# Seven block products for the up layer of a fused attention and maxout kernel, in half-batch units interleaved with the down layer

## The chip, the cores and the metric

One core of one Trainium2 chip. The metric is device time in microseconds (us) of the whole program, launch to end. A profile shows a span about 2 us shorter, from the first to the last instruction.

PE is the matmul engine (PEld its weight loads), DVE the vector engine, ACT the scalar engine, POOL the engine that issues loads, SP the queue that issues stores and transposes.

A bank is a piece of PSUM, the memory that PE writes to; here it holds 128 x 512 numbers of fp32. A relief is the copy, relu or add on ACT or DVE that reads a finished product out of its bank, so that PE can write there again. A g sum or an x sum is one of the sums of blocks that the scheme below makes beforehand, of the up layer's output (g) or of x. A row is one line of a profile view.

## The reference, cut to what matters

```
k_proj = E @ k;  v_proj = F @ v                # per batch (8) and head (8); seq 1024, head_dim 64
attn   = softmax(q @ k_proj.T / 8) @ v_proj    # k_proj has 64 rows
x      = attn, heads side by side              # 8192 x 512
out    = max(x @ w1, x @ w2) @ w_out           # w1, w2: 512 x 1024; w_out: 1024 x 512
```

Both kernels use max(h1, h2) = h2 + relu(h1 - h2). So they make wd = w1 - w2 and m = w2 @ w_out once, and compute out = relu(x @ wd) @ w_out + x @ m. The first factor is the up layer, the rest the down layer.

## The kernel before

A batch is 1024 tokens. The up layer is plain: for each half batch and each of eight column blocks, four matmuls with 512 columns into one of four PSUM banks, then a relu into `gt`.

```python
def up_slots(t, j, banks=None, on_act=()):
    for fb in range(NFB):                                   # 8
        def up(fb=fb):
            h_ps = mm_bank(...)
            for r in range(NDC):                            # 4
                nc.tensor.matmul(out=h_ps, lhsT=wd_sb[:, r, fb * 128 : (fb + 1) * 128],
                                 rhs=t["xt"][:, r, :, j * W : (j + 1) * W], ...)
            # fb in on_act: relu on ACT; otherwise on DVE
        yield up
```

The down layer of batches 1 to 7 already uses a block scheme (Strassen's, in Winograd's form): the product of two 2 x 2 block matrices with seven block products instead of eight, for sums of blocks made beforehand on DVE (`step_s`) and sums of results made afterwards. Each of two groups goes through seven products of twelve matmuls with 256 columns. A product adds onto the bank that holds an earlier one, after that one has been copied out:

```python
def keep(g, name, bank):
    x = ppool.tile([128, 512], FP32, tag="p", name="p_sb")
    nc.scalar.copy(out=x, in_=bank)
order = (p1, 0), (p2, 0), (p1, 1), (p2, 1), (p5, 0), (p6, 0), (p3, 0), (p7, 0), (p5, 1), \
    (p4, 0), (p6, 1), (p3, 1), (p7, 1), (p4, 1)
```

In a batch all up products come first, then all down products. The next batch's attention is cut into small steps (`step_sc` scores, `step_da` sums and weighted values, four pairs of heads) between them. `step_da` issues on ACT a logarithm and, straight after, an exponential that makes the inverse of the softmax sums; the multiply on DVE comes one product later.

The softmax here doesn't subtract the row's maximum and nothing guards it: scores larger than these inputs give would overflow.

Of the kernel before, what the change touches and what calls it, by code (L numbers as in the profile page):

```python
# [16 lines left out]
def kernel(  # L17
# [33 lines left out]
    xpool = ctx.enter_context(tc.tile_pool(name="xpool", bufs=2))  # L51
    gpool = ctx.enter_context(tc.tile_pool(name="gpool", bufs=1))
# [13 lines left out]
    def att_banks():  # L66
        return ps.tile([128, 2, 512], FP32, tag="att", bufs=2, name="att_ps")
# [102 lines left out]
    def step_kv(t, h0=0, h1=H, which="kv", bank=None):  # L170
        kv_ps = mm_bank(n=bank)
# [23 lines left out]
    def step_kpt(t, h0=0, h1=H, n=None):  # L195
        kpt_ps = mm_bank(FP16, n)
        for h in range(h0, h1):
            for r in range(2):
                nc.tensor.transpose(  # L199
                    out=kpt_ps[r * D : (r + 1) * D, (h - h0) * KP : (h - h0 + 1) * KP],  # L200
                    in_=t["kp"][:, h, :],
                    identity=ident16[:KP, :KP],
                )
        nc.vector.tensor_copy(
            out=t["kpt"][:, h0:h1, :].rearrange("q h k -> q (h k)"),
            in_=kpt_ps[:, 0 : (h1 - h0) * KP],
        )
# [44 lines left out]
    def step_da(t, p):  # L252
# [18 lines left out]
        nc.scalar.activation(out=ld, in_=ld, func=ACTF.Exp, scale=-1.0)  # L271
        rec = ld

        def finish():
            nc.vector.tensor_tensor(  # L275
                out=t["xt"][:, p, :, :], in0=at_ps, in1=rec, op=ALU.mult
            )

        return finish
# [69 lines left out]
    def up_slots(t, j, banks=None, on_act=()):  # L349
        t["gt", j] = gt = gpool.tile([128, NFB, HALF], FP16, tag=f"gt{j}", name="gt_sb")  # L350
        for fb in range(NFB):
            def up(fb=fb):
                h_ps = mm_bank(n=None if banks is None else banks[fb % 4])
# [7 lines left out]
                if fb in on_act:  # L361
                    nc.scalar.activation(out=gt[:, fb, :], in_=h_ps, func=ACTF.Relu)  # L362
                else:
                    nc.vector.tensor_scalar_max(gt[:, fb, :], h_ps, 0.0)  # L364
# [68 lines left out]
    NK = NFB // 2 + NDC // 2  # L433
    CH = DM // 2

    def a_block(t, j, h, n):
        if n < NFB // 2:
            return t["gt", j][:, h * NFB // 2 + n, :].rearrange("q (o n) -> q o n", o=2)
        return t["xt"][:, h * NDC // 2 + n - NFB // 2, :, j * W : (j + 1) * W]

    def b_block(h, c):
        def chunk(n):
            cols = slice(c * CH, (c + 1) * CH)
            if n < NFB // 2:
                return wo_sb[:, h * NFB // 2 + n, cols]
            return m_sb[:, h * NDC // 2 + n - NFB // 2, cols]
        return chunk

    T_sb = const.tile([128, 4, NK, CH], FP16)

    def step_t(part):
        if part == 0:
            n0, n1, src = 0, NFB // 2, wo_sb
        else:
            n0, n1, src = NFB // 2, NK, m_sb
        hs = n1 - n0
        blk = lambda h, c: src[:, h * hs : (h + 1) * hs, c * CH : (c + 1) * CH]
        T = [T_sb[:, i, n0:n1, :] for i in range(4)]
        for out_, x, y in (
            (T[0], blk(0, 1), blk(0, 0)),  # L460
            (T[1], blk(1, 1), T[0]),
            (T[2], blk(1, 1), blk(0, 1)),
            (T[3], blk(1, 0), T[1]),
        ):
            nc.vector.tensor_tensor(out=out_, in0=x, in1=y, op=ALU.subtract)


    def step_s(t, which, part):
        if "S" not in t:
            t["S"] = [  # L470
                big(i)[:, 0 : NK * HALF].rearrange("q (n o m) -> q n o m", n=NK, o=2)
                for i in range(4)
            ]
        if part == 0:
            n0, n1 = 0, NFB // 2
            blk = lambda j, h: t["gt", j][:, h * n1 : (h + 1) * n1, :].rearrange(
                "q n (o m) -> q n o m", o=2)
        else:
            n0, n1 = NFB // 2, NK
            hs = NDC // 2  # L480
            blk = lambda j, h: t["xt"][:, h * hs : (h + 1) * hs, :, j * W : (j + 1) * W]
        S = [x[:, n0:n1, :, :] for x in t["S"]]
        for i in which:
            x, y, op = (
                (blk(1, 0), blk(1, 1), ALU.add),
                (S[0], blk(0, 0), ALU.subtract),
                (blk(0, 0), blk(1, 0), ALU.subtract),
                (blk(0, 1), S[1], ALU.subtract),
            )[i]
            for n in range(n1 - n0) if part else (slice(0, n1 - n0),):  # L490
                nc.vector.tensor_tensor(out=S[i][:, n], in0=x[:, n], in1=y[:, n], op=op)  # L491

    def down_steps(b, t):
        A = lambda j, h: lambda n: a_block(t, j, h, n)
        Sb = lambda i: lambda n: t["S"][i][:, n, :, :]
        Tb = lambda i: lambda n: T_sb[:, i, n, :]
        prods = {
            1: (A(0, 0), b_block(0, 0)), 2: (A(0, 1), b_block(1, 0)), 3: (Sb(3), b_block(1, 1)),
            4: (A(1, 1), Tb(3)), 5: (Sb(0), Tb(0)), 6: (Sb(1), Tb(1)), 7: (Sb(2), Tb(2)),
        }  # L500
        st = [{}, {}]

        def product(g, k, name, first):
            if first:
                st[g][name] = mm_bank(n={"X": (0, 2), "Y": (1, 3), "Z": (1, 3)}[name][g])
            bank = st[g][name]
            a, w_ = prods[k]
            for i in range(2):
                for n in range(NK):
                    nc.tensor.matmul(  # L510
                        out=bank[:, i * CH : (i + 1) * CH],
                        lhsT=a(n)[:, g, i * 128 : (i + 1) * 128],
                        rhs=w_(n),
                        start=(first and i == 0 and n == 0), stop=(n == NK - 1), skip_group_check=True,
                    )
            return bank

        def keep(g, name, bank):
            x = ppool.tile([128, 512], FP32, tag="p", name="p_sb")
            nc.scalar.copy(out=x, in_=bank)  # L520
            st[g][name] = x
# [4 lines left out]
        def o_tile(g, j):  # L526
            st[g]["o", j] = opool.tile([128, 2, DM], FP32, tag="o", name="o_sb")

        def add(g, j, c, x, y):
            nc.vector.tensor_tensor(  # L530
                out=cols(st[g]["o", j], c), in0=two(x), in1=two(y), op=ALU.add)

        def store(g, j):
            nc.sync.dma_start(
                out=out.rearrange("(n p i o) m -> n o p i m", p=128, i=NI, o=2)[
                    b, g, :, 2 * j : 2 * j + 2, :
                ],
                in_=st[g]["o", j],
            )

        def p1(g):
            keep(g, "s1", product(g, 1, "X", True))

        def p2(g):
            bank = product(g, 2, "Y", True)
            o_tile(g, 0)
            add(g, 0, 0, bank, st[g]["s1"])

        def p5(g):
            keep(g, "s5", product(g, 5, "Z", True))  # L550

        def p6(g):
            keep(g, "u2", product(g, 6, "X", False))

        def p3(g):
            add(g, 0, 1, product(g, 3, "Z", False), st[g]["u2"])
            store(g, 0)

        def p7(g):
            keep(g, "u3", product(g, 7, "X", False))  # L560
            o_tile(g, 1)
            add(g, 1, 1, st[g]["u3"], st[g]["s5"])

        def p4(g):
            bank = product(g, 4, "X", False)
            nc.scalar.copy(out=cols(st[g]["o", 1], 0), in_=two(bank))  # L566
            store(g, 1)

        order = (p1, 0), (p2, 0), (p1, 1), (p2, 1), (p5, 0), (p6, 0), (p3, 0), (p7, 0), (p5, 1), \
            (p4, 0), (p6, 1), (p3, 1), (p7, 1), (p4, 1)  # L570
        return [lambda f=f, g=g: f(g) for f, g in order]

# [54 lines left out]
    for b in range(1, B):  # L627
        t = tiles[b]
        banks = None if b == 1 else (0, 1, 3, 2)
        seq = [*up_slots(t, 0, banks, (2, 6)), *up_slots(t, 1, banks, (2, 6))]  # L630
        seq += down_steps(b, t)
        own = [((b, n), x) for n, x in enumerate(seq)]
        if b > 1:
            last = slots.pop()
            own[2:2] = [last]
        slots += own
# [3 lines left out]
    def at_slot(b, n, s, *a):  # L640
        steps.setdefault((b, n), []).append(lambda: s(*a))

    for b in range(1, B):
        t = tiles[b]
        at = lambda n, s, *a: at_slot(b - 1, n, s, t, *a)
        if b == 1:
            at(19, new_attn)
            plan = "kv 19, kpt 20, qt0 21, qt1 23, sc0 24, da0 26, qt2 27, sc1 29, da1 31, " \
                "qt3 32, sc2 33, da2 35, sc3 37, da3 39"
        elif b == 2:  # L650
            at_slot(0, 33, new_attn, t)
            at_slot(0, 33, step_qt_dma, t, 0, H // 2)
            at_slot(0, 36, step_qt_dma, t, H // 2, H)
            plan = "kv 1, kpt 2, sc0 4, da0 6, sc1 8, da1 10, sc2 12, da2 14, sc3 16, da3 19"
        else:
            at_slot(b - 2, 7, new_attn, t)
# [67 lines left out]
```

## Time and profile before

| | before |
|---|---|
| time | 357.81 us median of 3 (356.91 to 358.63) |
| span of the profile | 354.6 us, of a run of 356.39 us |
| period of a batch | 39.37 us |
| PE, DVE, ACT busy in a period | 39.13, 25.45, 20.62 us |
| wait of PE in a period | one, 0.24 us |

The period is read from equal places of successive batches in the chain that ended last (167.71, 207.08, 246.45). A PE that is busy 39.13 of 39.37 us says that only fewer or shorter matmuls can help, and that any wait the change adds counts in full.

### The profile page before, as it was taken

The page shows a single profiled execution, that of the slowest core. Times are in us where ns is not written, and L with a number is a line of the kernel's source. Part 1 is how long each engine was busy: PE and PEld are TensorE (multiplying, and loading weights), DVE is VectorE, ACT ScalarE, POOL GpSimd, SP SyncE. Part 2 cuts the span into 40 slices and gives each one's busy share as a digit, 9 for nine tenths or more (in the row PEclk, how much of TensorE's full clock was granted, in tenths as well). Part 3 has the DMA queues.
Part 4 walks back from the last instruction along what each step waited for, and adds up shares of the span by engine and source line. Part 5 has one row for each costly group of instructions (what it writes and reads, how often), then busy time and mean ns, then how long its engine had stood idle before and what let it go on. Part 6 is the DMA issues. An engine that isn't in the chain of part 4 may idle for free.

```text
span 354.6 us, 6214 instructions
## 1 busy us (share of the span) xinstructions
PE 343.9 (97%) x2667; PEld 203.2 (57%) x2667; DVE 209.9 (59%) x312; ACT 169.5 (48%) x219; POOL 31.4 (9%) x43
## 2 busy tenths in 40 slices
PE   8998999999999999999999999999999999999994
PEld 3544444434368644875368635874377635874783
DVE  1367707326894469734992579635972589538911
ACT  2438123772755376536564376436663375432131
POOL 8332001002000100010000100000000000000000
PEclk9999999999999999999999999999999999999999
DMA  8999999999996999849973897869502210031014
GB/s 151 205 195 202 207 207 183 247 152 235 200 204 92 248 255 167 116 134 197 234 118 95 164 254 119 118 154 219 105 2 98 82 59 2 33 146 59 2 66 173
DMA packets 65068, 52.31 MB, mean 148 GB/s; under 512 B 26000, under 2 KB 56720, under 8 KB 65040
## 3 DMA queue, kind: packets, MB, share of 16 engines
q0 software_dynamic: 31312, 28.31, 52.6%
q1 hardware_dynamic: 33728, 23.60, 24.9%
q8 instruction: 21, 0.34, 0.4%
q14 instruction: 7, 0.06, 0.1%
HBM read 57.15 MB, written 16.78 MB: 208 GB/s over the span
## 4 chain that ended last, share of the span: by engine, by line
PE 88%; DMA 4%; DVE 3%; POOL 2%; ACT 1%; issue 1%; DVEq 0%; POOLq 0%
PE mm_ps L510 37%; PE mm_ps L355 31%; PE mm_ps L384 6%; DMA big<-in_moe_w_dram 4%; PE mm_ps L178 4%; PE att_ps L263 3%; PE att_ps L239 3%; PE mm_ps L424 2%; DVE o_sb L530 1%; PE mm_ps L199 1%; DVE gt_sb L364 1%; PE mm_ps L215 1%; POOL q_sb L100 0%; POOL v_sb L100 0%; DVE wd_sb L402 0%
## 5 line engine op out<-in xcount | busy, mean ns | idle before, releaser
L355 PE MATMUL mm_ps<-xt_sb,wd_sb 128*128 128x512 f16 x512 | 119.9, 380 | 1.6 <-DVE wd_sb L402 1.1
L355 PEld LDWEIGHTS <-wd_sb 128*128 128x128 f16 x512 | 46.7, 98 | 63.6 <-issue 13.6
L364 DVE TENSOR_SCALAR gt_sb<-mm_ps 128x512 f16<-128x512 f32 x100 | 67.5, 686 | 26.0 <-PE mm_ps L355 25.8
L510 PEld LDWEIGHTS <-big 128*128 128x128 f16 x672 | 64.9, 98 | 13.3 <-issue 3.7
L520 ACT COPY p_sb<-mm_ps 128x512 f32<-128x512 f32 x56 | 32.7, 584 | 65.2 <-PE mm_ps L510 60.1
L510 PE MATMUL mm_ps<-T_sb,big 128*128 128x256 f16 x504 | 59.7, 273 | 1.3 <-DVE o_sb L530 1.2
L275 DVE TENSOR_TENSOR xt_sb<-att_ps,ld_sb 128x1024 f16<-128x1024 f32 x28 | 34.2, 1223 | 27.1 <-ACT ld_sb L271 27.1
L270 ACT ACTIVATE ld_sb<-att_ps 128x1024 f32<-128x1024 f32 x28 | 28.7, 1024 | 21.6 <-PE att_ps L263 21.6
L510 PEld LDWEIGHTS <-gt_sb 128*128 128x128 f16 x336 | 32.4, 98 | 9.0 <-issue 2.7
L510 PE MATMUL mm_ps<-wo_sb,gt_sb 128*128 128x256 f16 x224 | 33.7, 273 | 0.2 <-DVE gt_sb L364 0.2
L530 DVE TENSOR_TENSOR o_sb<-mm_ps,p_sb 128x512 f32<-128x512 f32 x28 | 18.8, 688 | 22.5 <-PE mm_ps L510 22.4
L247 ACT ACTIVATE ex_sb<-att_ps 128x1024 f16<-128x1024 f32 x28 | 28.7, 1025 | 6.1 <-PE att_ps L239 5.1
L271 ACT ACTIVATE ld_sb<-ld_sb 128x1024 f32<-128x1024 f32 x28 | 29.6, 1058 | 0.9
L362 ACT ACTIVATE gt_sb<-mm_ps 128x512 f16<-128x512 f32 x28 | 16.6, 594 | 20.8 <-PE mm_ps L355 20.8
L191 DVE CAST vp_sb<-mm_ps 64x512 f16<-64x512 f32 x7 | 4.9, 695 | 29.5 <-ACT kp_sb L187 29.5
L510 PE MATMUL mm_ps<-m_sb,xt_sb 128*128 128x256 f16 x112 | 21.4, 273 | 0.0
L530 DVE TENSOR_TENSOR o_sb<-p_sb 128x512 f32<-128x512 f32 x14 | 9.7, 693 | 17.0 <-ACT p_sb L520 17.0
L100 POOL DMA_DIRECT2D v_sb<-in_v_dram x9 | 7.6, 852 | 129.9 <-DMA qt_sb<-q_sb 105.6
L510 PEld LDWEIGHTS <-xt_sb 128*128 128x128 f16 x168 | 16.4, 98 | 1.9
L510 PE MATMUL mm_ps<-T_sb,gt_sb 128*128 128x256 f16 x112 | 16.8, 272 | 0.7 <-ACT p_sb L520 0.7
L491 DVE TENSOR_TENSOR big<-gt_sb 128x2048 f16<-128x2048 f16 x14 | 17.1, 1220 | 0.6
L566 ACT COPY o_sb<-mm_ps 128x512 f32<-128x512 f32 x14 | 8.2, 587 | 18.9 <-PE mm_ps L510 18.9
(72 smaller groups left out, 330.3 us busy)
## 6 DMA issues: line engine op xcount, KB each, us to landing
out_dram<-o_sb SPq DMA_DIRECT2D x28, 512.0 KB, 2.8
k_sb<-in_k_dram POOLq DMA_DIRECT2D x7, 1024.0 KB, 18.6
v_sb<-in_v_dram POOLq DMA_DIRECT2D x7, 1024.0 KB, 9.7
q_sb<-in_q_dram POOLq DMA_DIRECT2D x7, 1024.0 KB, 13.5
big<-in_moe_w_dram POOLq DMA_DIRECT2D x8, 256.0 KB, 14.4
out_dram<-o_sb SPq DMA_DIRECT2D x8, 256.0 KB, 4.5
k_sb<-in_k_dram POOLq DMA_DIRECT2D x2, 512.0 KB, 7.9
v_sb<-in_v_dram POOLq DMA_DIRECT2D x2, 512.0 KB, 12.6
```

Source lines behind the costliest of these rows:

```text
L247: nc.scalar.activation(out=ex, in_=sc_ps, func=ACTF.Exp, scale=scale)
L270: nc.scalar.activation(out=ld, in_=dn_ps, func=ACTF.Ln)
L271: nc.scalar.activation(out=ld, in_=ld, func=ACTF.Exp, scale=-1.0)
L275: nc.vector.tensor_tensor(out=t["xt"][:, p, :, :], in0=at_ps, in1=rec, op=ALU.mult)
L355: nc.tensor.matmul(out=h_ps, lhsT=wd_sb[:, r, fb * 128 : (fb + 1) * 128], rhs=t["xt"][:, r, :, j * W : (j + 1) * W], start=(r == 0), stop= ...
L362: nc.scalar.activation(out=gt[:, fb, :], in_=h_ps, func=ACTF.Relu)
L364: nc.vector.tensor_scalar_max(gt[:, fb, :], h_ps, 0.0)
L384: nc.tensor.matmul(out=op_ps, lhsT=lhsT, rhs=rhs, start=(n == 0), stop=(n == NFB + NDC - 1),)
L491: nc.vector.tensor_tensor(out=S[i][:, n], in0=x[:, n], in1=y[:, n], op=op)
L510: nc.tensor.matmul(out=bank[:, i * CH : (i + 1) * CH], lhsT=a(n)[:, g, i * 128 : (i + 1) * 128], rhs=w_(n), start=(first and i == 0 and n ...
L520: nc.scalar.copy(out=x, in_=bank)
L530: nc.vector.tensor_tensor(out=cols(st[g]["o", j], c), in0=two(x), in1=two(y), op=ALU.add)
```

## The change

The intent: take the up layer's matmul time down by an eighth with the same seven-product scheme, and hide the extra copies and sums by putting two short up products of the next unit (half a batch) behind each down product of this one. The core of the diff, with cuts:

```diff
-    xpool = ctx.enter_context(tc.tile_pool(name="xpool", bufs=2))
-    gpool = ctx.enter_context(tc.tile_pool(name="gpool", bufs=1))
+    xpool = ctx.enter_context(tc.tile_pool(name="xpool", bufs=3))
+    gpool = ctx.enter_context(tc.tile_pool(name="gpool", bufs=2))
 ...
-        nc.scalar.activation(out=ld, in_=ld, func=ACTF.Exp, scale=-1.0)
+        def invert():                       # run one product later; finish one after that
+            nc.scalar.activation(out=ld, in_=ld, func=ACTF.Exp, scale=-1.0)
+            return finish
 ...
+    units = [(b, o) for b in range(1, B) for o in range(2)]
+    def up_steps(u):
+        for d in range(2):                  # two column pairs
+            xbank, ybank = (2, 3) if d == 0 else (3, 2)
+            # product(k, ...): for m in range(2): for n_ in range(NX): one matmul of 256 columns
+            def p1(...): st["s1"] = keep("pu", product(1, "X", xbank))
+            def p2(...): add(0, 0, product(2, "Y", ybank), st["s1"]); relu(c_blk(0, 0))
+            def p6(...): st["u1"] = keep("pu", product(6, "X", None))
+            def p5(...): st["s5"] = keep("pu", product(5, "Z", ybank))
+            def p7(...): st["u2"] = keep("pu", product(7, "X", None))
+            def p3(...):
+                add(0, 1, product(3, "Z", None), st["u1"])
+                add(1, 1, st["u2"], st["s5"])
+                relu(u["gt"][:, NG + 2 * d : NG + 2 * d + 2, :])
+            def p4(...): UP_C21(out=c_blk(1, 0), in_=two(product(4, "X", None)))   # relu on ACT
+            yield from (p1, p2, p6, p5, p7, p3, p4)
 ...
+        for i, x in enumerate(downs):       # seven down products of this unit
+            r = (key[0], 7 * key[1] + i)
+            slots.append((r + (0,), x))
+            slots += [(r + (1 + m,), y) for m, y in enumerate(ups[2 * i : 2 * i + 2])]
```

Down products take banks 0 and 1, up products 2 and 3; the projection of k and v and its transposes move to attention's banks. The first unit's up layer stays plain. "Slot" below is one down product with the two up products behind it; a batch has slots 0 to 13.

## The prediction

> **What bounds the kernel now.** I read the page from the top: busy shares, slices, the chain that ended last. Then the windows view over one batch period, the groups by form in that period, PE's waits, and the timeline of PE, ACT and DVE.
>
> ```profile
> PE 343.9 (97%) x2667; PEld 203.2 (57%) x2667; DVE 209.9 (59%) x312; ACT 169.5 (48%) x219; POOL 31.4 (9%) x43
> ...
> PEclk9999999999999999999999999999999999999999
> ...
> PE 88%; DMA 4%; DVE 3%; POOL 2%; ACT 1%; issue 1%; DVEq 0%; POOLq 0%
> PE mm_ps L510 37%; PE mm_ps L355 31%; PE mm_ps L384 6%; DMA big<-in_moe_w_dram 4%; PE mm_ps L178 4%; PE att_ps L263 3%; PE att_ps L239 3%; PE mm_ps L424 2%; DVE o_sb L530 1%; PE mm_ps L199 1%; DVE gt_sb L364 1%; PE mm_ps L215 1%; POOL q_sb L100 0%; POOL v_sb L100 0%; DVE wd_sb L402 0%
> ```
>
> The chain runs through PE for 88% of the span: the down layer's seven products (L510) and the up layer (L355) are 68% of it. The clock is full, so matmul work taken away gives time back, unless something else then makes PE wait. Three neighbouring batches and PE's waits after batch 0:
>
> ```profile
> 167.71:207.08 39.37, 39.13 (x315) 24.12 (x314) 25.45 (x38) 20.62 (x27) 2.62 (x3) 1.00 0.84 163
> 207.08:246.45 39.37, 39.13 (x313) 24.14 (x314) 25.45 (x38) 20.62 (x27) 1.75 (x2) 1.00 0.86 167
> 246.45:285.81 39.36, 39.13 (x313) 24.13 (x314) 25.44 (x38) 20.62 (x27) 0.00 (x0) 1.00 0.31 84
> ```
> ```profile
> PE mm_ps L510 <- DVE o_sb L530: 1.2, 5, 0.2
> PE mm_ps L510 <- ACT p_sb L520: 0.7, 1, 0.7
> PE mm_ps L510 <- DVE gt_sb L364: 0.2, 1, 0.2
> ```
>
> Columns of the first: span, then PE, PEld, DVE, ACT, POOL busy, clock, DMA share. A batch lasts 39.37 us; PE is busy 39.13 of it and waits once, 0.24 us; DVE is 65% and ACT 52% busy. Shares of DMA differ (0.86, then 0.31) at equal periods, so transfers are hidden.
>
> Spacing, not the duration of one record, is what a matmul costs. From starts in the timeline of PE:
>
> ```profile
> 207.01 2.76 PE L355 MATMUL mm_ps<-xt_sb,wd_sb 128*128 128x512 f16 x12
> 209.71 0.41 PE L263 MATMUL att_ps<-ex_sb,ones 64*64 64x512 f16 x4
> ...
> 225.00 2.78 PE L510 MATMUL mm_ps<-T_sb,big 128*128 128x256 f16 x24 [0.24 <-DVE o_sb L530]
> 227.61 0.60 PE L510 MATMUL mm_ps<-wo_sb,big 128*128 128x256 f16 x4
> ```
>
> 24 matmuls of 256 columns take 227.61 - 225.00 = 2.61 us, 0.109 each. Twelve of 512 take 2.70 us with about 0.1 lost at the switch to 64-row tiles, 0.216 each (the chain has 56 in 12.09 us, also 0.216). Halving columns thus halves cost, with weight loads hidden.
>
> **What the Trainium skill says.** "TensorE: Matmul & The Clock Gate", Back-to-back issue gap, gives N/2.4 + 2.5 ns for an isolated gap: 109 ns at 256 and 216 at 512. The trace agrees with those; it does not agree with the lower sustained 131 ns at N=512 named there.
> "ScalarE: Activation LUTs", What ACT_TABLE_LOAD costs, says back-to-back ACTIVATEs overlap by about 93 ns. The trace agrees: a PSUM copy lasts 0.59 us but the next exponential started 0.48 us after it (219.86, 220.34), and three DVE reliefs of 128x512 took 1.88 us, 0.60 apiece instead of 0.69. I use 0.48 and 0.95 us for ACT, 0.60 and 1.14 for DVE where ready work is queued.
> "VectorE: DVE Perf Modes", the perf-mode tier table: tensor_scalar on 16-bit SBUF data runs at up to 4x, tensor_tensor at 2x, fp32 from PSUM at 1x. The trace shows the last two (1024 fp16: 0.69 us; 512 fp32: 0.69); it has no SBUF relu, so I estimate 0.29 us for 512 and 0.42 for 1024 from that page's 150 cycles plus N/4.
> "PSUM — Partial Sum Buffer", Engine vs sequencer instructions: the ACT and DVE queues are strict FIFO. That decides the new waits below.
>
> **The change, part by part.**
> 1. Up layer on PE. A unit is 512 tokens, half a batch. Before, 32 matmuls x 0.216 = 6.91 us. After, two column pairs x seven products x four matmuls = 56 x 0.109 = 6.12 us (0.1092 unrounded). That is 0.80 us a unit. Of 14 units the first stays plain: 13 x 0.80 = 10.4 us, all on the bound engine. The down layer keeps 84 matmuls a unit, attention its count and its ten insertions a batch; weight-load switches do not grow, since up and down products now have one shape.
> 2. ACT per batch. Up reliefs were 4 of 16; now 20 copies or relus (four kept products and one direct relu per column pair). With 10 for the down layer: 30 x 0.48 = 14.4 us, attention 4 x (0.95 + 0.95 + 1.0) = 11.6, the kp cast 0.5: 26.5 us against a period of about 37.5, 71%.
> 3. DVE per batch. Up adds 12, down adds 6: 18 x 0.60 = 10.8; relus 4 x (0.29 + 0.42) = 2.8; sums of x 8 x 0.35 = 2.8, of g 8 x 0.63 = 5.0; attention 4 x 1.14 = 4.6; casts and kpt 1.7. Sum 27.7 us, 74%. Neither becomes the bound on average.
> 4. Waits removed: the 0.24 us wait on the o_sb add comes from two down groups changing phase together; here a down bank is reused two products and four up products later. 5 x 0.24 = 1.2. The 0.7 us at the last product goes too, since the last unit alone alternates two banks with 1.3 us between: 0.7.
> 5. Weight differences of the up layer: four DVE ops of 1024 fp16, 2.8 us once, beside batch 0's down matmuls, where DVE has idle gaps of over 2 us. Nothing on the path.
> 6. Waits added. A slot is a down product (12 x 0.109 = 1.31 us) and two up products (0.44 each): 2.18 us, 2.5 to 2.8 with attention. An up bank is taken again about 1.75 us after its product ended, so its relief may start about 1.1 us late. I walked the FIFO orders of ACT and DVE through the 14 slots of a batch. Only one spot overruns: in slot 8 the logarithm and deferred inverse of attention pair 0 follow the up copies. In us from the slot's start, the sums end at 1.31 + 0.44 + 0.1, ACT starts the logarithm at 2.33, the next copy at 3.29, the inverse at 3.77, ending 4.83. DVE has the normalising multiply first in its queue (4.88 to 6.02), then a g sum (to 6.62), an x sum (to 6.96), and only then the add that frees the bank of up product 3, ending 7.65. PE wants that bank for the next column pair at 2.84 + 2.18 + 1.31 + 0.44 + 0.44 = 7.2. So 0.5 us, in the five batches 1 to 5 that carry pair 0 of a later batch there: 2.5 us. I add 1.0 us for small ones in the dense stretch of batch 1 and elsewhere that the walk, good to about 0.2 us a step, would not show.
> Sum: 357.8 - 10.4 - 1.9 + 3.5 = 349.0 us. Head and tail (first loads, last store) are the same.
>
> **The rivals.**
> A. *Nothing waits.* Then 357.8 - 10.4 - 1.9 = 345.5. For it: average loads of 71 and 74%, banks and buffers separated (three x tiles, two g tiles, own pools for kept up and down products). Against: those are averages; one of three slots has over 3 us of attention on ACT.
> B. *FIFO bunching costs more than my walk.* DVE's raw rows would fill about 31 of 37.5 us; if neighbouring instructions overlap less than 0.09 us, backlog lasts over several slots and each column pair of each unit waits 0.2 to 0.4 us, 26 x 0.3 = 8 us in place of 3.5: 353.5. Against: the 0.60 us spacing is regular in the trace, and the lightest slots carry under 1 us of DVE work, so backlog drains.
> C. *Transfers emerge.* All three loads of a batch are now issued together, and q's transposes and stores share one queue. Rows: k lands in a median 18.6 us, v 9.7, q 13.5; transposes 10.5. Needed about 31 us later; hidden. If q came late, a transpose would block the stores behind it and, with three output tiles, PE: 355 or more. I give this 5%.
> D. *Smaller matmuls pay a switching cost.* No: the down layer already runs mixed sources at 0.109.
>
> **Range and chances.** The saving of 10.4 is arithmetic on measured spacing, good to 0.5. The waits are the doubt: 0 in A, 8 in B. Centre 349.0; 8 in 10 between 346.0 and 353.0. The 2% mark is 357.8 x 0.98 = 350.7, which needs waits of no more than 5.2 us; I hold that likely but not safe: 0.70 faster, 0.29 within, 0.01 slower.
>
> **What would show it.** Right: the up group in the 128x256 form, spacing 0.109, 13 x 56 matmuls; a batch period near 37.9 us in batches 2 to 5, and near 37.4 without new waits; DVE and ACT busy about 80% by rows; PE's longest wait an up product waiting for the DVE add into gt_sb, about 0.5 us, five times. Wrong: period over 38.5 with many waits of PE on p_sb or gt_sb (B); PE waiting on qt_sb or o_sb, SP's queue held by q_sb (C); spacing above 0.115 (D); or waits under 1 us in total (A).

## The result, and the profile after

The median was 347.3 us (346.84 to 349.01, 4 runs) against 357.52 for the kernel before in the same rounds; the ratio is 0.972, 95% interval 0.968 to 0.976. A ratio is the mean time of one kernel's runs over that of the other's of the same rounds, so not quite the ratio of the medians. In a second set of rounds the ratio was 0.974 (0.973 to 0.975), 347.2 against 356.6 us. Outputs were correct in every run below, one of which is the changed kernel again.

The page of the profile after:

```profile
PE 332.9 (96%) x2979; PEld 233.5 (68%) x2979; DVE 232.4 (67%) x394; ACT 218.7 (63%) x325; POOL 31.5 (9%) x43
...
PE 75%; DVE 9%; ACT 6%; DMA 6%; POOL 2%; issue 1%; DVEq 0%; ACTq 0%; POOLq 0%
```

PE has 312 matmuls more and 11.0 us less of busy time. ACT went from 48% to 63%, DVE from 59% to 67%. The chain that ended last leaves PE more often: some of its links are now reliefs that end at about the time when PE needs the bank. That alone is no lost time. Lost time is in PE's waits. Here are two neighbouring batches in the windows view (columns: span, then PE, PEld, DVE, ACT, POOL busy, clock, DMA share, GB/s), then the two longest kinds of wait of PE that are not in the head (total, times, longest):

```profile
160.00:197.90 37.90, 37.44 (x364) 28.81 (x360) 28.67 (x50) 27.87 (x44) 2.63 (x3) 1.00 0.88 169
197.90:235.80 37.90, 37.44 (x364) 28.83 (x360) 28.67 (x50) 27.87 (x44) 1.84 (x2) 1.00 0.82 155
```
```profile
PE mm_ps L552 <- DVE gt_sb L567: 2.6, 6, 0.5
...
PE mm_ps L630 <- DVE big L496: 0.3, 1, 0.3
```

Five of the six waits are the same spot of batches 1 to 5, which also gives the period: 198.46 - 160.52 = 37.94 us. The timeline that leads to that spot (start, length, instruction, idle time before it and what ended it): the start of slot 8 on PE, then ACT's logarithm, copy and inverse, then PE in slot 10:

```profile
152.79 0.60 PE L630 MATMUL mm_ps<-wo_sb,gt_sb 128*128 128x256 f16 x4
...
155.22 1.03 ACT L272 ACTIVATE ld_sb<-att_ps 128x1024 f32<-128x1024 f32 x1
156.13 0.59 ACT L506 COPY p_sb<-mm_ps 128x512 f32<-128x512 f32 x1
156.60 1.08 ACT L275 ACTIVATE ld_sb<-ld_sb 128x1024 f32<-128x1024 f32 x1
...
159.13 0.60 PE L552 MATMUL mm_ps<-xt_sb,big 128*128 128x256 f16 x4
159.66 0.41 PE L241 MATMUL att_ps<-qt_sb,kpt_sb 64*64 64x512 f16 x4
160.52 0.60 PE L552 MATMUL mm_ps<-xt_sb,wd_sb 128*128 128x256 f16 x4 [0.46 <-DVE gt_sb L567]
```

The scores at 159.66 are normally followed by the next product after 0.34 us (190.28 after 189.94, in the next batch). Here it is 0.86. So PE loses 0.52 us where the row says 0.46: a row's idle time counts from the modelled end of the last matmul, which lies behind the moment at which the next could have been issued. DVE around the same spot one batch later:

```profile
195.65 1.22 DVE L279 TENSOR_TENSOR xt_sb<-att_ps,ld_sb 128x1024 f16<-128x1024 f32 x1 [1.78 <-ACT ld_sb L275]
196.79 0.68 DVE L496 TENSOR_TENSOR big<-gt_sb,big 128x1024 f16<-128x1024 f16 x1
...
197.39 0.42 DVE L496 TENSOR_TENSOR big<-xt_sb 128x512 f16<-128x512 f16 x1
...
197.72 0.68 DVE L567 TENSOR_TENSOR gt_sb<-mm_ps,p_sb 128x512 f16<-128x512 f32 x1
...
198.46 0.60 PE L552 MATMUL mm_ps<-xt_sb,wd_sb 128*128 128x256 f16 x4 [0.46 <-DVE gt_sb L567]
```

DVE stands idle for 1.78 us until ACT has made the inverse (released by L275), then does the multiply, a g sum, an x sum, and only then the add of up product 3 that frees PE's bank. The up product that it frees starts 0.06 us after the add ends. This is the queue order that the prediction had walked through, and its times hold. Counted from the start of slot 8 at 152.79, the logarithm starts at 2.43 us, the copy at 3.34 and the inverse at 3.81, ending at 4.89; the walk had 2.33, 3.29, 3.77 and 4.83. PE is ready for the bank at 160.00, which is 7.21 us (walk: 7.2), and gets it at 7.73.

### The profile page after: what moved, and what is told of

Read it like the earlier page. It is cut to its first block, busy times and chain, and to the rows that moved or that the text cites. A ratio compares the mean times of both kernels' runs of the same rounds, so it can differ in the third digit from the quotient of the medians.

```text
span 345.4 us, 7094 instructions
## 1 busy us (share of the span) xinstructions
PE 332.9 (96%) x2979; PEld 233.5 (68%) x2979; DVE 232.4 (67%) x394; ACT 218.7 (63%) x325; POOL 31.5 (9%) x43
## 4 chain that ended last, share of the span: by engine, by line
PE 75%; DVE 9%; ACT 6%; DMA 6%; POOL 2%; issue 1%; DVEq 0%; ACTq 0%; POOLq 0%
PE mm_ps L630 31%; PE mm_ps L552 21%; PE mm_ps L385 5%; DMA big<-in_moe_w_dram 4%; PE mm_ps L359 4%; PE att_ps L265 4%; PE att_ps L180 3%; DVE big L496 2%; PE att_ps L241 2%; DVE xt_sb L279 2%; ACT ld_sb L272 2%; DVE gt_sb L567 2%; PE mm_ps L425 2%; ACT ld_sb L275 2%; PE mm_ps L520 2%
## 5 line engine op out<-in xcount | busy, mean ns | idle before, releaser
L506 ACT COPY p_sb<-mm_ps 128x512 f32<-128x512 f32 x160 | 89.1, 592 | 44.0 <-PE mm_ps L630 29.6
L630 PEld LDWEIGHTS <-big 128*128 128x128 f16 x672 | 65.7, 98 | 8.1 <-DVE big L496 0.5
L630 PE MATMUL mm_ps<-T_sb,big 128*128 128x256 f16 x504 | 61.6, 273 | 0.3 <-DVE big L496 0.3
L567 DVE TENSOR_TENSOR gt_sb<-mm_ps,p_sb 128x512 f16<-128x512 f32 x52 | 35.8, 689 | 22.4 <-PE mm_ps L552 22.4
L552 PEld LDWEIGHTS <-big 128*128 128x128 f16 x416 | 38.9, 98 | 12.7 <-issue 8.5
L552 PE MATMUL mm_ps<-big 128*128 128x256 f16 x312 | 43.7, 273 | 0.3 <-DVE gt_sb L567 0.3
L552 PEld LDWEIGHTS <-wd_sb 128*128 128x128 f16 x312 | 28.2, 98 | 13.8 <-issue 10.7
L552 PE MATMUL mm_ps<-xt_sb,wd_sb 128*128 128x256 f16 x208 | 31.0, 273 | 2.3 <-DVE gt_sb L567 2.3
L275 ACT ACTIVATE ld_sb<-ld_sb 128x1024 f32<-128x1024 f32 x28 | 30.0, 1070 | 0.4
L570 DVE TENSOR_SCALAR gt_sb<-gt_sb 128x512 f16<-128x512 f16 (+1 forms) x52 | 19.1, 367 | 1.8
L496 DVE TENSOR_TENSOR big<-gt_sb 128x1024 f16<-128x1024 f16 x28 | 19.2, 685 | 0.9
L567 DVE TENSOR_TENSOR gt_sb<-p_sb 128x512 f16<-128x512 f32 x26 | 17.7, 681 | 0.0
```

What stands on the lines that cost most here:

```text
L275: nc.scalar.activation(out=ld, in_=ld, func=ACTF.Exp, scale=-1.0)
L496: nc.vector.tensor_tensor(out=S(i), in0=x, in1=y, op=op)
L552: nc.tensor.matmul(out=bank[:, m * W : (m + 1) * W], lhsT=w_[:, n_, (2 * d + m) * 128 : (2 * d + m + 1) * 128], rhs=a[:, n_, :], start=(n ...
L567: nc.vector.tensor_tensor(out=c_blk(j, c), in0=two(x), in1=two(y), op=ALU.add)
L570: nc.vector.tensor_scalar_max(ap, ap, 0.0)
L630: nc.tensor.matmul(out=bank[:, i * CH : (i + 1) * CH], lhsT=a(c)[:, i * 128 : (i + 1) * 128], rhs=w_(c), start=(n is not None and i == 0 a ...
```

## The experiments

The theory: the time is PE's stream of matmuls plus the waits for banks that the FIFO orders of DVE and ACT make; seven products take about 10 us from the stream, and interleaving keeps the waits small. Two rivals: the gain comes from the new order, not from fewer matmul columns; or ACT and DVE, now some 75% busy in a period, set the time by their load, and the one visible wait is only a symptom.

| run | median us | ratio to before, 95% interval |
|---|---|---|
| changed kernel, again | 347.17 | 0.974 (0.973 to 0.975) |
| bank first | 344.84 | 0.967 (0.966 to 0.968) |
| extra sum in slot 9 | 351.02 | 0.985 (0.983 to 0.986) |
| extra sum in slot 3 | 347.31 | 0.974 (0.973 to 0.976) |
| plain up units | 354.18 | 0.994 (0.993 to 0.996) |
| not interleaved | 396.08 | 1.111 (1.109 to 1.112) |
| inverse at once | 351.53 | 0.986 (0.984 to 0.987) |

All seven ran on one chip, beside 9 to 10 runs of the kernel before, median 356.6 us.

### The changed kernel again

> The changed kernel unaltered, as the yardstick for the three runs beside it. Ratio to the kernel before 0.972 within 0.004, about 347.3 us; PE waits 0.46 us for the DVE add into gt_sb in the same place of five batches.

Measured: 347.17 us, and the same six waits of 2.6 us in total. It is the yardstick for the others.

### Bank first

```diff
-            where = tuple(((b - 1, k, 1), i) for k, i in ((8, 2), (9, 0), (10, 1), (11, 3)))
+            where = tuple(((b - 1, k, 1 + (k == 9)), i) for k, i in ((8, 2), (9, 0), (10, 1), (11, 3)))
-        for key, i in (end, 0), ((b, r, 0), 1), ((b, r + 1, m), 2), ((b, r + 2, m), 3):
+        for key, i in (end, 0), ((b, r, 0), 1), ((b, r + 1, m), 2), ((b, r + 2, m + m * o), 3):
```

> In the second unit of each batch a g sum and an x sum are issued after the adds of up product 3 instead of before them, so that the add that frees the PSUM bank no longer stands behind them in the DVE queue. My theory (the 0.46 us wait is made by the order of the DVE queue): all five waits go, 5 x 0.46 = 2.3 us less than the changed kernel, about 345.0 us, ratio 0.965. Rival (the wait is set by the late inverse on ACT, with the normalising multiply as the last link, whatever stands behind it): under 0.5 us gained. Rival (DVE and ACT are so full that the wait comes up elsewhere): five waits of another line, time unchanged.

Measured: 344.84 us, 2.33 less. DVE and PE at the spot:

```profile
194.33 1.23 DVE L279 TENSOR_TENSOR xt_sb<-att_ps,ld_sb 128x1024 f16<-128x1024 f32 x1 [1.79 <-ACT ld_sb L275]
...
195.47 0.68 DVE L567 TENSOR_TENSOR gt_sb<-mm_ps,p_sb 128x512 f16<-128x512 f32 x1
...
196.62 0.61 PE L552 MATMUL mm_ps<-xt_sb,wd_sb 128*128 128x256 f16 x4
...
197.13 0.69 DVE L496 TENSOR_TENSOR big<-gt_sb,big 128x1024 f16<-128x1024 f16 x1
```

DVE still waits 1.79 us for the inverse, but the add now follows the multiply, and the product starts without a wait. All five waits are gone and none took their place; what is left on this line is one of 0.3 us in batch 6. Both rivals fall as they were put: with the inverse as late as before and the same load, another order is enough. The late inverse is still part of the cause, since the run with the inverse at once (below) loses these five waits too, without this change of order. The period is 37.43 us (in equal places, 218.82 - 181.39). This version beats both kernels.

### An extra sum, in slot 9 and in slot 3

```diff
             at_slot(key, sums_g, u, (i,))
+        if o == 1 and b <= 5:                  # the other run: o == 0, key (b, 3, 0)
+            at_slot((b, 9, 1), sums_g, u, (3,))
```

In slot 9:

> The same g sum is issued a second time (same result) just before the add that frees the bank, in batches 1 to 5. My theory: each wait grows by the spacing of one such op, 0.60 to 0.68, so 0.46 becomes about 1.1 us, five times: +3.0 to 3.4 us over the changed kernel, about 350.5. Rival (the wait is set by ACT or by something other than the DVE queue): under 0.5 us more.

In slot 3:

> The same extra g sum, five times as well, but issued in the fourth slot of the first unit, where DVE has the least to do. My theory (only the queue's order in front of a bank matters, the total load of DVE does not): no change, within 0.3 us of the changed kernel. Rival (DVE's load as such sets the time of the attention stretch): the same +3 us as in the other place.

Measured: +3.85 us in slot 9, +0.14 us in slot 3, where the intervals of the two ratios overlap almost wholly. PE's waits with the sum in slot 9:

```profile
123.61 0.60 PE L552 MATMUL mm_ps<-xt_sb,wd_sb 128*128 128x256 f16 x4 [1.18 <-DVE gt_sb L567]
...
162.27 0.60 PE L552 MATMUL mm_ps<-xt_sb,wd_sb 128*128 128x256 f16 x4 [1.18 <-DVE gt_sb L567]
```

Each wait grew by 0.72 us, not 0.60 to 0.68: the trace has the two sums in one row of 1.41 us, so they do not overlap as neighbours on DVE mostly do. That the second writes the tile that the first wrote is the likely reason; it was not tested. With the same DVE work added to both runs, one pays in full and the other not at all. So DVE's total load does not set the time at these two places; its order in front of a bank does.

### Plain up units

Units, interleaving, buffers and deferred inverse stay; each unit's up layer is eight plain products in banks 2 and 3.

```diff
-        ups = [*up_steps(U[units[n + 1]])] if n + 1 < len(units) else []
+        ups = [*up_plain_units(U[units[n + 1]])] if n + 1 < len(units) else []
+ ...        # in words: product fb is 4 matmuls 128x512 into mm_bank(n=2 + fb % 2); relu on ACT if fb % 2 else on DVE
```

> Half-batch units, interleaving, buffers and the deferred inverse as in the changed kernel, but the up layer of all units as eight plain products of four 128x512 matmuls, alternating two banks and relieved half by ACT and half by DVE. My theory (the gain is the 10.4 us of matmul time): the 10.4 us come back, the five waits of 0.46 us go since no add stands in front of a bank, 347.3 + 10.4 - 2.3 = 355.4 us, ratio 0.994; the batch period is about 39.1 us. Rival (most of the gain is the new order, that is units, interleaving and no wait at the end of products): under 350 us, ratio below 0.98.

Measured: 354.18 us. The period, from two starts of the k and v projection:

```profile
185.86 0.40 PE L180 MATMUL att_ps<-k_sb,eft 128*64 128x512 f16 x1
...
224.87 0.40 PE L180 MATMUL att_ps<-k_sb,eft 128*64 128x512 f16 x1
```

That is 39.01 us. PE has no recorded wait after the first plain products of batch 1. With seven products and no wait, in the bank-first run, the period is 37.43: 1.58 us less, where the prediction's arithmetic gives 2 x 0.80. With the bank-first run this splits the change into three measured steps: 356.6 to 354.2, -2.4 us, for the new order without fewer matmuls (units, interleaving, buffers and the deferred inverse together); 354.2 to 344.8, -9.3 us, for the seven products; 344.8 to 347.2, +2.3 us, for the five waits. The rival that the order makes the gain keeps a quarter of it.

### Not interleaved

```diff
-        for i, x in enumerate(downs):
-            r = (key[0], 7 * key[1] + i)
-            slots.append((r + (0,), x))
-            slots += [(r + (1 + m,), y) for m, y in enumerate(ups[2 * i : 2 * i + 2])]
+        for i, r in enumerate(rs):
+            slots += [(r + (1 + m,), y) for m, y in enumerate(ups[2 * i : 2 * i + 2])]
+        slots += [(r + (0,), x) for r, x in zip(rs, downs)]
```

Attention's steps were moved behind down products, and the sums were moved to where their inputs are ready.

> Both layers as seven products, but the fourteen up products of the next unit are issued all together, then the seven down products of this unit; attention's scores and sums go between down products, and some sums move to stay in order. My theory (interleaving is what gives a bank 1.75 us to be relieved in): an up product lasts 0.44 us, so a bank is wanted again 0.44 us after its product ended while relief takes 0.11 + 0.6 + 0.05 us; by the walk about 0.17 us of wait for each of 13 x 14 products, 31 us, so about 375 us, ratio 1.05. Rival (the fewer matmuls alone give the gain; ACT and DVE work at 65% load would hide in any order): under 352 us.

Measured: 396.08 us. The direction is right, and the rival that the order does not matter is out. The size is not: +49 us instead of +28. PE and ACT within one run of up products, with its first column pair from 186.30 and its second from 191.55:

```profile
186.30 1.05 PE L552 MATMUL mm_ps<-xt_sb,wd_sb 128*128 128x256 f16 x8
186.55 1.03 ACT L249 ACTIVATE ex_sb<-att_ps 128x1024 f16<-128x1024 f32 x1
...
187.47 0.59 ACT L506 COPY p_sb<-mm_ps 128x512 f32<-128x512 f32 x1
...
188.11 1.87 PE L552 MATMUL mm_ps<-big 128*128 128x256 f16 x12 [0.76 <-ACT p_sb L506]
...
191.55 1.03 PE L552 MATMUL mm_ps<-xt_sb,wd_sb 128*128 128x256 f16 x8 [0.31 <-DVE gt_sb L567]
...
192.19 0.59 ACT L506 COPY p_sb<-mm_ps 128x512 f32<-128x512 f32 x1 [0.31 <-PE mm_ps L552]
...
192.82 1.87 PE L552 MATMUL mm_ps<-big 128*128 128x256 f16 x12 [0.24 <-ACT p_sb L506]
...
194.82 0.60 PE L552 MATMUL mm_ps<-big,wd_sb 128*128 128x256 f16 x4
...
195.80 0.60 PE L630 MATMUL mm_ps<-wo_sb,gt_sb 128*128 128x256 f16 x4
```

In the second pair only the products' own reliefs are in the way. The first product's four matmuls are issued by 191.55 + 0.44 = 191.99; its copy starts at 192.19, 0.20 us later, where the walk had 0.11. The three products from 192.82 take 2.00 us, 0.67 each, instead of 0.44.

The fourteen up products of this unit take from 186.30 to 195.80 in PE's timeline, 9.5 us instead of 56 x 0.1092 = 6.12. The thirteen units, read in the same way, are together 48.9 us over, so the loss lies in the up products.

Not all of it is waits for banks. In the first pair the third product starts 1.81 us after the first, in the second pair 1.27: the copy at 187.47 stands behind attention's exponential. In six other units PE waits in the first pair for x sums that this run had moved:

```profile
PE mm_ps L552 <- DVE big L496: 7.1, 6, 1.2
```

The last unit has neither in front of it; it takes 9.02 us (361.81 to 370.83), 2.90 over. As an estimate, 13 x 2.90 = 38 us of the 49 are waits for banks, 0.21 us a product where the walk had 0.17, and about 11 us come from the attention steps and sums that this run also moved. No run measured these shares apart. Recorded waits of PE add up to less than 30 us in this profile, again because each row's idle time is shorter than the loss.

### Inverse at once

```diff
-        def invert():
-            nc.scalar.activation(out=ld, in_=ld, func=ACTF.Exp, scale=-1.0)
-            return finish
+        nc.scalar.activation(out=ld, in_=ld, func=ACTF.Exp, scale=-1.0)
-        return invert
+        return finish
```

> The inverse of the softmax sums is issued on ACT straight after the logarithm again, ahead of the copy of the up product that follows, as in the kernel before. My theory: the wait of 0.46 us in slot 9 goes because the multiply runs earlier, but three of four attention pairs put the logarithm and the inverse, 2.0 us, in front of the copy that frees a bank: about 0.4 us of PE wait on p_sb each, 5 batches x (3 x 0.4 - 0.46) = +3.7 us, about 351 us, ratio 0.982. Rival (the order of two ACT instructions does not matter at 63% load): 345 to 347.5 us.

Measured: 351.53 us, +4.4. ACT and PE where pair 0 is worked on:

```profile
156.58 1.03 ACT L272 ACTIVATE ld_sb<-att_ps 128x1024 f32<-128x1024 f32 x1
157.64 1.06 ACT L274 ACTIVATE ld_sb<-ld_sb 128x1024 f32<-128x1024 f32 x1
158.60 1.54 ACT L504 COPY p_sb<-mm_ps 128x512 f32<-128x512 f32 x3
```
```profile
158.30 0.60 PE L550 MATMUL mm_ps<-big 128*128 128x256 f16 x4
159.22 0.60 PE L550 MATMUL mm_ps<-big,wd_sb 128*128 128x256 f16 x4 [0.32 <-ACT p_sb L504]
```

Logarithm and inverse hold ACT for 2.0 us; the copy that frees the bank starts only at 158.60, and product 3 comes 0.92 us after product 7 instead of 0.44. There are fifteen such waits, three in each of five batches, while the waits on the add into gt_sb are gone. The rows give 4.4 us for the fifteen; that this equals the +4.4 measured is chance, since the rows leave out a part and the 2.3 us of the old waits come off. From start to start the three of a batch cost 0.48, 0.34 and 0.53 us; less the 0.52 of the wait that went, 0.83 is left. The period is 38.78 us (159.22 to 198.00, same place), 0.84 more than with the deferred inverse, and 5 x 0.84 = 4.2. So deferring the inverse by one product is a needed part of the change.

## Why the prediction was right

- The matmul term, -10.4 us: the two runs that differ on PE in the up layer alone (plain units and bank first) give -9.3, or -9.8 by the spans of their profiles (352.3 and 342.5). The rest fits small waits that only the seven products have: rows of 0.35 us in batch 6 and 0.26 us in the last unit, nearer 0.9 us together with the 0.16 us or so that a row leaves out after a 256-column product. The spacing is 0.109 as forecast: 333.73 to 337.67 for 36 matmuls. Nothing was lost to switching between up and down products: a down product and the two up products behind it start at 155.63, 156.94, 157.38 and the next at 157.82, which is 1.31, 0.44 and 0.44 us.
- Waits removed, -1.9 us: the new order alone gives -2.4. The term was a little small: it left out the third wait of its own list (0.2 us on gt_sb) and took the rows at face value, though rows leave out a part. The rest of the new order was not measured apart.
- The wait added in slot 10, 0.5 us in five batches: 0.46 in the row, 0.52 from starts, in these five batches and at this product. Order, place and times are those of the walk, so this is no luck. Taking it away gave 2.33 us of the 2.5 forecast.
- Small waits, +1.0 us: these were found in batch 6 and in the last unit, not in the dense stretch of batch 1, where PE has no recorded wait beyond the first plain products. That they come to about the forecast 1.0 us is luck, as it was an allowance for what the walk would not show. The prediction names no wait in batch 6. The other batches have the k and v projection in slot 5; batch 6 has none there, so up product 5 comes sooner than the add that frees its bank. That is read from the trace; no run took it away.
- Load of ACT and DVE: 27.87 and 28.67 us of 37.90 by rows, 74 and 76%, against "about 80%". In the two places tried, the time did not follow DVE's load as such. The two relus, which the trace before did not have, took 294 ns for 512 and 427 ns for 1024 numbers of fp16, against the 0.29 and 0.42 us estimated with "VectorE: DVE Perf Modes", the perf-mode tier table.
- The period: 37.94 against 37.9, and 37.43 without the five waits against 37.4.
- Rival A (nothing waits) forecast 345.5; the bank-first version shows that state at 344.8, and the change as given missed it by its five waits. Rival B (bunching everywhere) would have shown many waits; the rows show six. Rival C (transfers) did not come up: in batch 1 and after, no wait of PE is on a transfer. Rival D is out by the spacing.
- The total, 349.0 against 347.3: of the 1.7 us, some is the yardstick. The runs of before beside the later set had a median of 356.6, and the sum's -8.8 us from there is 347.8.

What did fail is the size in one expectation, that of the not-interleaved run, +49 us for +28. Its wait for banks, 0.17 us a product, came out nearer 0.21 (the start of a relief, 0.11 us after the product in the walk, measured 0.20), which is about 7 us in all. It left out what its own moved sums and attention steps put in front of reliefs, about 11 us. Both are estimates from the trace.

## What to carry to other kernels

Cutting matmul work paid on this PE-bound kernel because each bank's relief had time, and two short products behind each long one bought that time: without interleaving the same products cost 49 us more, an estimated 38 of them in waits for banks. Averages of 75% on ACT and DVE did not show where PE would wait; walk their FIFO queues from one bank to its next use, and issue the op that frees a bank ahead of sums that are needed later. Take lost PE time from start to start, not from the idle time of a row.

## What the Trainium skill lacked or had wrong

- "TensorE: Matmul & The Clock Gate", Back-to-back issue gap: it gives 131 ns a matmul as the sustained rate at N=512 for a stream of weight loads and matmuls, and calls its formula N/2.4 + 2.5 an isolated gap. In this kernel's long streams the formula is the sustained rate: 216 ns at 512 columns (56 in 12.09 us) and 109 at 256.
- The same page, Single matmul latency, (398 + N)/2.4, gives 272 ns at 256 columns, as the rows do (273). No page gives the times around a relief: from the issue end of a product's last matmul to the start of its copy 0.20 us, from the end of a relief to the matmul it frees 0.04 to 0.06 us. In the not-interleaved run these and the copy of 0.59 us make 0.83 us, of which the product in the other bank covers 0.44.
- "Perfetto Trace Analysis", Optimization Strategy, advises to look for gaps between slices on the busy engine. Elsewhere the page calls PE's end an estimate, but it does not say how far that shortens the gaps. Here they came out too small: 0.46 us shown for 0.52 lost after a scores group, 0.32 for 0.48 after a 256-column product.
